# Top-k attention with a gated feed-forward: the 32nd largest score found by a fold into larger and smaller halves

## The chip, the cores and the metric

The kernel runs on one core of one Trainium2 chip. The metric is the device time of one execution in microseconds, the median of several. Of the core's engines five matter here: TensorE (PE, with its weight loads shown apart as PEld), VectorE (DVE), ScalarE (ACT), GpSimd (POOL) and the queues that issue transfers (SP foremost).

## The reference

Attention over 8 batches of 8 heads, 576 tokens and 64 dimensions a head, keeps for each query the 32 largest of its 576 scores; the rest get no weight. Its output, brought into 4608 rows of 512, goes through a feed-forward of 2048 hidden units with the activation h·cos(h). All is float32.

```python
# attention: q, k, v of (8, 8, 576, 64)
scores = scale * np.matmul(q, k.transpose(0, 1, 3, 2))
kth = np.partition(scores, -top_k, axis=-1)[..., -top_k:-top_k + 1]   # top_k = 32
mask = scores >= kth
scores = np.where(mask, scores, -1000000000.0)
scores = scores - np.max(scores, axis=-1, keepdims=True)
attn = np.exp(scores)
attn = attn / (np.sum(attn, axis=-1, keepdims=True) + 1e-09)
out = np.matmul(attn, v)
# feed-forward: x of (4608, 512), w_in (512, 2048), w_out (2048, 512)
h = x @ w_in
g = h * np.cos(h)
y = g @ w_out
```

## The kernel before

The work is cut into 144 units: 128 queries (one to a partition) by two heads. A unit's scores are 2 x 576 numbers a partition. The program is written as slots; in each one, every engine gets a piece of a different unit, and feed-forward pieces ("feed") fill TensorE's time. In the long middle (`slot`), slot i runs the top-k of unit i on VectorE, mask and exponentials of unit i-1 on ScalarE, normalisation and transposition of the units before on GpSimd and by transfers, and scores of unit i+1 on TensorE.

The scores come out in PSUM and are copied to SBUF by ScalarE; after that copy the PSUM tile (one buffer, `bufs=1`) is free for the next unit's scores:

```python
def scores(u):
    sc = u["sc"] = ps.tile([P, 2, 2, 512], F32, tag="sc", name="sc", bufs=1)
    ...
    nc.tensor.matmul(sc[r0 : r0 + rows, j, h, 0:HS], ...)      # HS = 288, h = 0, 1

def take_scores(u):
    s = u["s"] = work.tile([P, 2, S], F32, tag="s", name="s", bufs=4)
    nc.scalar.copy(out=s..., in_=u.pop("sc")...[:, :, 0:HS])
```

The top 32 are found in four rounds. Each takes the eight largest in order (`max`, MAX8 in the profile) and overwrites them by the lowest number (`match_replace`: a MATCH_VALUE_LOAD and a MATCH_REPLACE8), for each of the two heads; the last round needs no replacement. The 32nd value is the threshold, the first is the maximum:

```python
def topk_round(u, rnd):
    s = u["s"]
    if rnd == 0:
        u["m8"] = small.tile([P, 2, TOPK], F32, tag="m8", name="m8")
        u["rest"] = work.tile([P, 2, S], F32, tag="rest", name="rest", bufs=1)
    m8, rest = u["m8"], u["rest"]
    src = s if rnd == 0 else rest
    at = slice(8 * rnd, 8 * rnd + 8)
    for j in range(2):
        nc.vector.max(m8[:, j, at], src[:, j])                                    # L237
    if rnd < TOPK // 8 - 1:
        for j in range(2):
            nc.vector.match_replace(rest[:, j], m8[:, j, at], src[:, j], NEG)     # L240
    else:
        del u["rest"]

def bounds(u):
    m8 = u.pop("m8")
    nb = u["nb"] = small.tile([P, 2, 2], F32, tag="nb", name="nb")
    nc.scalar.mul(out=nb, in_=m8[:, :, 0 : TOPK : TOPK - 1], mul=-SCALE)          # L248
    ...
```

The order of a slot in the middle (z holds two units in every other slot, else nothing):

```python
def slot(i, u, w, x, y, z):
    if x: reciprocal(x)                      # DVE
    if u: topk_round(u, 0); decode_second(2) # DVE
    if w: bounds(w); mask(w); exponentials(w)        # ACT
    if u: topk_round(u, 1); topk_round(u, 2); topk_round(u, 3)   # DVE
    take_banks()                             # ACT: feed-forward banks
    if z: values(z)                          # PE
    if i + 1 < NU: scores(units[i + 1])      # PE
    if z: take_values(z)                     # ACT
    if i + 1 < NU: take_scores(units[i + 1]) # ACT
    ...
    gate(1)                                  # POOL: g * sine(x), L457
    if x: normalise(x); split(x); write_halves(x)    # POOL L282, L294, then SP
    feed(2)                                  # PE: feed-forward
    take_banks()
    ...
    reduce_first(); reduce_second()          # POOL L431 to L433, L440
    feed(3)                                  # PE
    sines(2)                                 # ACT
```

`decode_second` (L137, L138) is part of a decoding of the weights, on VectorE, in the first slots only. In the end, after the last slot, `reduce_first` and `gate` run on VectorE (L423, L426, L457) instead of GpSimd.

Of the kernel before, what the change touches and what calls it, by code (L numbers as in the profile page):

```python
# [10 lines left out]
F32 = mybir.dt.float32  # L11
# [3 lines left out]
AF = mybir.ActivationFunctionType  # L15
ALU = mybir.AluOpType

P = 128
TOPK = 32
NEG = -3.4028234663852886e38  # L20
# [11 lines left out]
def kernel(  # L32
# [9 lines left out]
    nc = tc.nc  # L42
    ctx.enter_context(tc.manual_schedule())
    B, H, D, S = qT.shape
# [6 lines left out]
    HS = S // 2  # L51
    SCALE = 1.0 / math.sqrt(D)
# [5 lines left out]
    work = ctx.enter_context(tc.tile_pool(name="work", bufs=2))  # L58
    small = ctx.enter_context(tc.tile_pool(name="small", bufs=4))
# [25 lines left out]
    for i in range(DF // CW):  # L85
        w = consts.tile([P, NC, CW], F32, tag=f"w_in{i}", name=f"w_in{i}")
        w_in.append(w)
        for c in range(NC):
            cols = slice(words * i * CW, words * (i + 1) * CW)
            chunks.append((moe_w_in[c * P : (c + 1) * P, cols], w[:, c]))  # L90
    for f in range(NF):
        w = consts.tile([P, DM], F32, tag=f"w_out{f}", name=f"w_out{f}")
# [62 lines left out]
    units = []  # L155
    for t0 in range(0, B * S, P):
        parts = []
# [63 lines left out]
    def take_scores(u):  # L221
        s = u["s"] = work.tile([P, 2, S], F32, tag="s", name="s", bufs=4)
        nc.scalar.copy(  # L223
            out=s.rearrange("p j (h w) -> p (j h) w", h=2),
            in_=u.pop("sc").rearrange("p j h w -> p (j h) w")[:, :, 0:HS],
        )

    def topk_round(u, rnd):
        s = u["s"]
        if rnd == 0:  # L230
            u["m8"] = small.tile([P, 2, TOPK], F32, tag="m8", name="m8")
            u["rest"] = work.tile([P, 2, S], F32, tag="rest", name="rest", bufs=1)
        m8, rest = u["m8"], u["rest"]
        src = s if rnd == 0 else rest
# [6 lines that stand above are left out]
        else:  # L241
            del u["rest"]

    def bounds(u):

        m8 = u.pop("m8")
        nb = u["nb"] = small.tile([P, 2, 2], F32, tag="nb", name="nb")
        nc.scalar.mul(out=nb, in_=m8[:, :, 0 : TOPK : TOPK - 1], mul=-SCALE)  # L248
        nd = u["nd"] = small.tile([P, 2], F32, tag="nd", name="nd")
        for j in range(2):  # L250
            nc.scalar.activation(
                out=nd[:, j : j + 1], in_=m8[:, j, TOPK - 1 : TOPK], func=AF.Identity,
                bias=nb[:, j, 0:1], scale=SCALE,
            )

    def mask(u):

        s, nb = u["s"], u.pop("nb")
        for j in range(2):
            nc.scalar.activation(  # L260
                out=s[:, j], in_=s[:, j], func=AF.Prelu, bias=nb[:, j, 1:2], scale=SCALE, alpha=FAR
            )
# [63 lines left out]
    def values(us):  # L326


        o = us[0]["o"] = ps.tile([P, 512], F32, tag="mm", name="o", bufs=4)
        for i, u in enumerate(us):  # L330
            pT = u.pop("pT")
            for b, _, rows, r0 in u["parts"]:
                st = pairs[b, u["hp"]]
                r = slice(r0, r0 + rows)
                to = slice(i * P + r0, i * P + r0 + rows)
                for c in range(NT + 1):
                    for j in range(2):
                        d = slice(j * D, (j + 1) * D)
                        if c < NT:
                            lhsT, rhs = st["v"][:, c, d], pT[:, j * (NT + 1) + c, r]  # L340
                        else:
                            lhsT, rhs = st["v_tail"][:, d], pT[:, NT, r]
                        nc.tensor.matmul(o[d, to], lhsT, rhs, start=c == 0, stop=c == NT)  # L343
# [35 lines left out]
    def ff1(blk, i):  # L379
        w = blk["w"]  # L380
        nf = 256 // w
        part = i % 4
        if part == 0:
            blk["g"].append(ffw.tile([P, 1024], F32, tag="g", name="g", bufs=CHUNKS))
            ff["live"] += 1
        if part % 2 == 0:
            blk["mm"] = ps.tile([P, 512], F32, tag="mm", name="mm", bufs=4)
        g, mm = blk["g"][-1], blk["mm"]
        for a in range(nf):
            f = i * nf + a  # L390
            at = (part % 2 * nf + a) * w
            for c in range(NC):
                nc.tensor.matmul(  # L393
                    mm[:, at : at + w],
                    w_in[f // FC][:, c, (f % FC) * P : (f % FC + 1) * P],
                    blk["xT"][:, c],
                    start=c == 0,
                    stop=c == NC - 1,
                )
        if part % 2 == 0:  # L400
            return
        full.append((take_first, blk, g, mm, part // 2))
# [6 lines left out]
    def take_banks():  # L409
        while full:  # L410
            take, *what = full.popleft()
            take(*what)
# [47 lines left out]
    def ff2(blk, i, f0):  # L460
        w = blk["w"]
        if f0 == 0:
            blk["o"] = ps.tile([P, 512], F32, tag="mm", name="o2", bufs=4)
        o = blk["o"]
        per = 1024 // w
        for f in range(f0, f0 + 2):
            g = blk["g"][f // per]
            at = (f % per) * w + i * P
            nc.tensor.matmul(  # L469
                o, g[:, at : at + P], w_out[f], start=f == 0, stop=f == NF - 1  # L470
            )
        if f0 + 2 < NF:
            return
        full.append((take_second, blk, i, o))
# [25 lines left out]
    def feed(n):  # L500

        ff["tick"] += 1
        while n > 0 and ff["credit"] >= 1:
            for kind in (ff["kind"], 1 - ff["kind"]):
                if (can_first, can_second)[kind]():
                    break
            else:
                return
            if kind == 0:
                ff1(*first.popleft())  # L510
            else:
                ff2(*second.popleft())
            ff["kind"] = 1 - kind
            n, ff["credit"] = n - 1, ff["credit"] - 1
# [10 lines left out]
    for n in range(NP, len(order)):  # L525
        i = last[order[n - 5]] - 1 if n >= 5 else 0
        at_slot.setdefault(max(i, NP + 2), []).append((load_qk, *order[n]))
        i = last[order[n - 6]] if n >= 6 else 0
# [8 lines left out]

    EARLY, LAST = 2 * NP, NU - NP

    def early_slot(i, u, w):  # L540
        n = 3 if i < 6 else 2
        topk_round(u, 0)
        decode_second(1 if i == 0 else n)
        scores(units[i + 1])
        for load, b, hp in at_slot.get(i, []):
            load(b, hp)
        load_weights(n)
        if w:
            bounds(w)
            mask(w)  # L550
            exponentials(w)
            reciprocal(w)
        topk_round(u, 1)
        if i == 0:
            decode_second(2)
        topk_round(u, 2)
        topk_round(u, 3)
        if w:
            normalise(w)
        take_banks()  # L560
        take_scores(units[i + 1])
        gate(1)
        decode_third()
        feed(2)
        reduce_first()
        reduce_second()
        if i != NP:
            decode_first(n - 1)
        if w:
            transposes_now(w)  # L570
        feed(1)
        decode_first(n - len(wq["second"]))
        if w:
            values([w])
            take_values([w])
        feed(2)
        sines(2)

    def slot(i, u, w, x, y, z):
        if x:  # L580
            reciprocal(x)
        if u:
            topk_round(u, 0)
            decode_second(2)
        if w:
            bounds(w)
            mask(w)
            exponentials(w)
        if u:
            topk_round(u, 1)  # L590
            topk_round(u, 2)
            topk_round(u, 3)
        take_banks()
        if z:
            values(z)
        if i + 1 < NU:
            scores(units[i + 1])
        if z:
            take_values(z)
        if i + 1 < NU:  # L600
            take_scores(units[i + 1])
        for load, b, hp in at_slot.get(i, []):
            load(b, hp)
        load_weights(2)
        if y:
            transposes(y)
        gate(1)
        if x:
            normalise(x)
            split(x)  # L610
            write_halves(x)
        feed(2)
        take_banks()
        decode_third()
        decode_first(2)
        reduce_first()
        reduce_second()
        feed(3)
        sines(2)
# [51 lines left out]
    for i in range(NU + 1):  # L671
# [4 lines left out]
        u, w = (units[i - n] if 0 <= i - n < NU else None for n in range(2))  # L676
# [55 lines left out]
```

## Time and profile before

| | |
|---|---|
| time, median of 3 | 1534.06 us (1532.54 to 1536.82) |
| span of the profiled execution | 1530.3 us, 28322 instructions |
| largest groups on GpSimd | L294 copy 2103 ns x132, L440 2372 ns x68, L457 2374 ns x68, L282 750 ns x288 |
| largest group on ScalarE | L268 exponentials 763 ns x288 |
| scores, L213 | 186.9 us busy, x1280 |

The profile is one execution taken by the hardware profiler. Its page gives busy times by engine, the chain of work that ended last, and the costliest groups of instructions: program line, engine, operation, output<-input, shapes, count, then busy us, mean ns of one instruction, and the idle time of the engine in front of them. The trace behind it can be asked for a timeline of one engine, or for busy times by stretch of time ("windows"). The length of an instruction includes latency that overlaps the next one, so what it costs a full engine is read from the distance between starts.

### The profile page before, as it was taken

How to read it: one execution, taken by the hardware profiler on the slowest of the kernel's cores; microseconds unless marked ns; L12 is line 12 of the kernel's file. 1: busy time of each engine (PE TensorE's matmuls, PEld its weight loads, DVE VectorE, ACT ScalarE, POOL GpSimd, SP SyncE). 2: the span in 40 equal slices, each digit the busy share in tenths (PEclk: the TensorE clock that was granted, in tenths of full speed). 3: DMA queues.
4: the chain of work that ended last, by engine and by line, in shares of the span. 5: the costliest groups of instructions: out<-in, count | busy, mean ns of one | idle time of the engine just before them, and what ended most of it. 6: DMA issues, size and time to landing. Idle time of an engine off the chain costs nothing.

```text
span 1530.3 us, 28322 instructions
## 1 busy us (share of the span) xinstructions
PE 1430.3 (93%) x10360; PEld 1022.7 (67%) x10360; DVE 1449.0 (95%) x3102; ACT 1109.6 (73%) x2150; POOL 1105.4 (72%) x838
## 2 busy tenths in 40 slices
PE   4678588999999999999999999999999999999998
PEld 3466266676767676767676767676767676767675
DVE  7999999999999999999999999999999999999911
ACT  7887667777777777777777777777777777777731
POOL 4778957777878787877777777777777778777600
PEclk6588899999999999999999999999999999999999
DMA  8432255645674556655565365645654446444200
GB/s 269 139 96 90 87 152 151 177 116 162 163 178 116 147 133 169 170 132 146 162 170 140 117 162 162 163 131 137 187 148 142 135 131 162 144 136 120 81 8 14
DMA packets 371740, 212.09 MB, mean 139 GB/s; under 512 B 321296, under 2 KB 337937, under 8 KB 371601
## 3 DMA queue, kind: packets, MB, share of 16 engines
q1 hardware_dynamic: 366192, 200.63, 48.4%
q10 hardware_dynamic: 5408, 9.65, 1.7%
q8 instruction: 81, 1.33, 0.4%
q14 instruction: 59, 0.48, 0.1%
HBM read 45.09 MB, written 87.29 MB: 87 GB/s over the span
## 4 chain that ended last, share of the span: by engine, by line
DVE 72%; PE 16%; ACT 5%; issue 5%; DMA 1%; POOL 0%; SPq 0%; ACTq 0%; POOLq 0%; DVEq 0%
DVE m L237 36%; DVE rest L240 33%; PE mm L393 6%; PE o L469 6%; PE o L343 2%; PE sc L213 1%; ACT s L268 1%; ACT s L260 1%; DVE w_out L138 1%; ACT st L127 1%; DVE rden L277 1%; DMA v<-in_v_dram 1%; ACT st L128 0%; PE tp L317 0%; DMA st<-in_moe_w_in_dram 0%
## 5 line engine op out<-in xcount | busy, mean ns | idle before, releaser
L393 PEld LDWEIGHTS mm<-xT,w_in 128*128 128x128 f32 x4608 | 546.6, 193 | 117.0 <-issue 95.2
L237 DVE MAX8 m<-rest 128x8 f32<-128x576 f32 x864 | 613.7, 757 | 0.0
L393 PE MATMUL mm<-xT,w_in 128*128 128x128 f32 x4608 | 567.0, 278 | 19.0 <-ACT xT L349 19.0
L469 PE MATMUL o<-w_out,g 128*128 128x512 f32 x1152 | 539.3, 600 | 11.5 <-POOL g L457 7.5
L240 DVE MATCH_REPLACE8 rest<-m,rest 128x576 f32<-128x576 f32 x576 | 426.4, 753 | 0.0
L469 PEld LDWEIGHTS o<-w_out,g 128*128 128x128 f32 x1152 | 202.7, 191 | 206.2 <-issue 190.7
L294 POOL COPY halves<-s 128x2304 uint16<-128x2304 uint16 x132 | 277.6, 2103 | 85.8 <-DMA rows<-halves 80.1
L282 POOL TENSOR_SCALAR s<-s,rden 128x576 f32<-128x576 f32 x288 | 212.3, 750 | 84.4 <-DVE rden L277 84.4
L268 ACT ACTIVATE s<-s,nd 128x576 f32<-128x576 f32 x288 | 219.5, 763 | 0.6
L240 DVE MATCH_REPLACE8 rest<-m,s 128x576 f32<-128x576 f32 x288 | 213.2, 753 | 0.0
L237 DVE MAX8 m<-s 128x8 f32<-128x576 f32 x288 | 203.1, 752 | 7.0 <-ACT s L223 7.0
L260 ACT ACTIVATE s<-s,nb 128x576 f32<-128x576 f32 x288 | 205.3, 760 | 0.0
L457 POOL TENSOR_TENSOR g<-g,x 128x1024 f32<-128x1024 f32 x68 | 161.4, 2374 | 57.3 <-ACT x L450 57.3
L213 PE MATMUL sc<-k,q 64*128 64x288 f32 (+1 forms) x1280 | 186.9, 439 | 14.5 <-ACT s L223 14.5
L223 ACT COPY s<-sc 128x1152 f32<-128x1152 f32 x144 | 160.6, 1115 | 39.9 <-PE sc L213 39.3
L343 PEld LDWEIGHTS o<-pT,v 128*64 128x64 f32 x2560 | 136.7, 141 | 69.2 <-issue 37.2
L343 PE MATMUL o<-pT,v 128*64 128x128 f32 (+1 forms) x2560 | 165.7, 272 | 14.3 <-ACT pT L321 8.4
L440 POOL TENSOR_TENSOR x<-g,x 128x1024 f32<-128x1024 f32 x68 | 161.3, 2372 | 5.7
L248 ACT ACTIVATE nb<-m 128x4 f32<-128x4 f32 x144 | 29.6, 206 | 185.3 <-DVE m L237 185.3
L405 ACT ACTIVATE g<-mm 128x512 f32<-128x512 f32 x144 | 84.3, 587 | 107.7 <-PE mm L393 107.7
L213 PEld LDWEIGHTS sc<-k,q 64*128 64x128 f32 (+1 forms) x1280 | 101.6, 182 | 66.5 <-ACT s L223 17.6
L431 POOL TENSOR_SCALAR x<-g 128x1024 f32<-128x1024 f32 x68 | 71.1, 1046 | 98.8 <-ACT g L405 94.0
(48 smaller groups left out, 1042.3 us busy)
## 6 DMA issues: line engine op xcount, KB each, us to landing
rows<-halves SPq DMA_DIRECT2D x132, 576.0 KB, 3.2
out_dram<-ob ACTq DMA_DIRECT2D x36, 256.0 KB, 2.1
q<-in_q_dram SPq DMA_DIRECT2D x31, 288.0 KB, 3.1
st<-in_moe_w_in_dram SPq DMA_DIRECT2D x16, 512.0 KB, 5.3
v<-in_v_dram SPq DMA_DIRECT2D x32, 256.0 KB, 3.5
st<-in_moe_w_out_dram SPq DMA_DIRECT2D x16, 512.0 KB, 3.6
k<-in_k_dram SPq DMA_DIRECT2D x31, 144.0 KB, 3.4
k<-in_k_dram SPq DMA_DIRECT2D x32, 128.0 KB, 3.9
```

Of the source, the lines that this page charges most:

```text
L213: nc.tensor.matmul(sc[r0 : r0 + rows, j, h, 0:HS], st["q"][d, q0 : q0 + rows], st["k"][d, h * HS : (h + 1) * HS], start=True, stop=True,)
L237: nc.vector.max(m8[:, j, at], src[:, j])
L240: nc.vector.match_replace(rest[:, j], m8[:, j, at], src[:, j], NEG)
L260: nc.scalar.activation(out=s[:, j], in_=s[:, j], func=AF.Prelu, bias=nb[:, j, 1:2], scale=SCALE, alpha=FAR)
L268: nc.scalar.activation(out=s[:, j], in_=s[:, j], func=AF.Exp, bias=nd[:, j : j + 1], scale=1.0, accum_out=den[:, j : j + 1],)
L282: nc.gpsimd.tensor_scalar(out=s[:, j], in0=s[:, j], scalar1=rden[:, j : j + 1], scalar2=1.0, op0=ALU.mult, op1=ALU.mult,)
L294: nc.gpsimd.tensor_copy(out=halves, in_=s.rearrange("p (k h) -> p h k", h=2))
L343: nc.tensor.matmul(o[d, to], lhsT, rhs, start=c == 0, stop=c == NT)
L393: nc.tensor.matmul(mm[:, at : at + w], w_in[f // FC][:, c, (f % FC) * P : (f % FC + 1) * P], blk["xT"][:, c], start=c == 0, stop=c == NC - 1,)
L440: nc.gpsimd.tensor_tensor(out=x, in0=g, in1=x, op=ALU.subtract)
L457: eng.tensor_tensor(out=g, in0=g, in1=x, op=ALU.mult)
L469: nc.tensor.matmul(o, g[:, at : at + P], w_out[f], start=f == 0, stop=f == NF - 1)
```

## The change

The 576 scores of a query are taken in pairs, score c of the left half with score c of the right half. VectorE writes the larger of each pair into the first 288 columns of `rest` and the smaller into the other 288 (`fold`). A pair can give both of its scores to the top 32 only if its smaller one belongs there, so at most 16 of the smaller ones can. The 32 largest of the larger ones (four rounds) and the 16 largest of the smaller ones (two rounds) therefore hold the top 32, in two ordered lists. The 32nd largest of both lists together is the largest of: the 32nd of the first list, and for n = 1 to 16 the lesser of the first list's entry 32-n and the second list's entry n. That is one `tensor_tensor` minimum, with the first list read backwards, and one reduction. The purpose is that the rounds run over half as many columns.

The left half is read from the PSUM tile of the scores, the right half from its copy in SBUF; the PSUM tile is therefore held until the fold has read it. Units 10 to 141 of 0 to 143 fold, the others keep the four rounds over 576. In slots without values to compute (`z` empty) a feed-forward piece now stands ahead of the next scores.

```diff
+        if not u["folds"]:
+            del u["sc"]          # in take_scores; otherwise the PSUM tile lives on
+
+    def fold(u):
+        s, sc = u["s"], u.pop("sc")
+        rest = u["rest"] = work.tile([P, 2, S], F32, tag="rest", name="rest", bufs=1)
+        for i, op in enumerate((ALU.max, ALU.min)):
+            nc.vector.tensor_tensor(
+                out=rest[:, :, i * HS : (i + 1) * HS], in0=sc[:, :, 0, 0:HS], in1=s[:, :, HS:S],
+                op=op,
+            )
 
     def topk_round(u, rnd):
+        if u["folds"]:
+            return folded_round(u, rnd)
...
+    def folded_round(u, rnd):
+        HALF = TOPK // 2
+        if rnd == 0:
+            fold(u)
+            u["m8"] = small.tile([P, 2, TOPK + HALF + 1], F32, tag="m8", name="m8", bufs=3)
+            u["ends"] = slice(0, TOPK + HALF + 1, TOPK + HALF)
+            u["low"] = small.tile([P, 2, HALF], F32, tag="low", name="low", bufs=1)
+        m8, low, rest = u["m8"], u["low"], u["rest"]
+        parts = [(m8[:, :, 8 * rnd : 8 * rnd + 8], slice(0, HS), rnd < TOPK // 8 - 1)]
+        if rnd < HALF // 8:
+            parts.append((low[:, :, 8 * rnd : 8 * rnd + 8], slice(HS, S), rnd < HALF // 8 - 1))
+        for to, cols, more in parts:
+            for j in range(2):
+                nc.vector.max(to[:, j], rest[:, j, cols])
+            if more:
+                for j in range(2):
+                    nc.vector.match_replace(rest[:, j, cols], to[:, j], rest[:, j, cols], NEG)
+        if rnd < TOPK // 8 - 1:
+            return
+        nc.vector.tensor_tensor(
+            out=m8[:, :, TOPK : TOPK + HALF], in0=m8[:, :, TOPK - 2 : TOPK - 2 - HALF : -1],
+            in1=low, op=ALU.min,
+        )
+        nc.vector.tensor_reduce(
+            out=m8[:, :, TOPK + HALF], in_=m8[:, :, TOPK - 1 : TOPK + HALF],
+            axis=mybir.AxisListType.X, op=ALU.max,
+        )
+        del u["rest"], u["low"]
...
+    for i, u in enumerate(units):
+        u["folds"] = EARLY + 2 <= i < LAST + 2        # EARLY = 8, LAST = 140
...
         take_banks()
         if z:
             values(z)
+        else:
+            feed(1)
         if i + 1 < NU:
             scores(units[i + 1])
```

More of the change, by code (lines that the diff above doesn't have):

```diff
@@ L224, in take_scores @@
             out=s.rearrange("p j (h w) -> p (j h) w", h=2),
-            in_=u.pop("sc").rearrange("p j h w -> p (j h) w")[:, :, 0:HS],
+            in_=u["sc"].rearrange("p j h w -> p (j h) w")[:, :, 0:HS],
         )
+        if not u["folds"]:
[8 more added lines that the diff above has]
+            )
     def topk_round(u, rnd):
+        if u["folds"]:
+            return folded_round(u, rnd)
         s = u["s"]
         if rnd == 0:
-            u["m8"] = small.tile([P, 2, TOPK], F32, tag="m8", name="m8")
+            u["m8"] = small.tile([P, 2, TOPK + TOPK // 2 + 1], F32, tag="m8", name="m8", bufs=3)
+            u["ends"] = slice(0, TOPK, TOPK - 1)
             u["rest"] = work.tile([P, 2, S], F32, tag="rest", name="rest", bufs=1)
@@ L242, in topk_round @@
             del u["rest"]
+    def folded_round(u, rnd):
[26 more added lines that the diff above has]
+        del u["rest"], u["low"]
     def bounds(u):
-        m8 = u.pop("m8")
+        m8, ends = u.pop("m8"), u.pop("ends")
         nb = u["nb"] = small.tile([P, 2, 2], F32, tag="nb", name="nb")
-        nc.scalar.mul(out=nb, in_=m8[:, :, 0 : TOPK : TOPK - 1], mul=-SCALE)
+        nc.scalar.mul(out=nb, in_=m8[:, :, ends], mul=-SCALE)
         nd = u["nd"] = small.tile([P, 2], F32, tag="nd", name="nd")
@@ L251, in bounds @@
             nc.scalar.activation(
-                out=nd[:, j : j + 1], in_=m8[:, j, TOPK - 1 : TOPK], func=AF.Identity,
+                out=nd[:, j : j + 1], in_=m8[:, j, ends.stop - 1 : ends.stop], func=AF.Identity,
                 bias=nb[:, j, 0:1], scale=SCALE,
```

## The prediction

> **What bounds the kernel now.** I read the page first: the table of engines, then the chain that ended last, then the costliest groups. Columns of a group: line, engine, operation, output<-input, shapes, count | busy us, mean ns of one | idle before it.
>
> ```profile
> PE 1430.3 (93%) x10360; PEld 1022.7 (67%) x10360; DVE 1449.0 (95%) x3102; ACT 1109.6 (73%) x2150; POOL 1105.4 (72%) x838
> ...
> DVE 72%; PE 16%; ACT 5%; issue 5%; DMA 1%; POOL 0%; SPq 0%; ACTq 0%; POOLq 0%; DVEq 0%
> ...
> L237 DVE MAX8 m<-rest 128x8 f32<-128x576 f32 x864 | 613.7, 757 | 0.0
> ...
> L240 DVE MATCH_REPLACE8 rest<-m,rest 128x576 f32<-128x576 f32 x576 | 426.4, 753 | 0.0
> ```
>
> Two engines are nearly full, and the chain runs 72% through VectorE (DVE): the top-k rounds, which never wait (idle 0.0). The windows view, cut into stretches, shows the long middle (columns: length, busy us and count for PE, PEld, DVE, ACT, POOL, then PE clock, DMA share, GB/s):
>
> ```profile
> 600.00:800.00 200.00, 198.24 (x1505) 144.36 (x1503) 200.00 (x435) 149.49 (x287) 152.06 (x113) 1.00 0.58 155
> ```
>
> DVE is busy for all 200 us, PE for 198, POOL (GpSimd) for 152. One unit (128 queries, two heads) in the DVE timeline (start us, length, then the instruction):
>
> ```profile
> 741.60 0.17 DVE L277 RECIPROCAL rden<-den 128x2 f32<-128x2 f32 x1
> 741.66 1.42 DVE L237 MAX8 m<-s 128x8 f32<-128x576 f32 x2
> 742.98 0.09 DVE L240 MATCH_VALUE_LOAD rest<-m,s 128x8 f32 x1
> 743.04 0.76 DVE L240 MATCH_REPLACE8 rest<-m,s 128x576 f32<-128x576 f32 x1
> 743.70 0.10 DVE L240 MATCH_VALUE_LOAD rest<-m,s 128x8 f32 x1
> ...
> 751.30 0.16 DVE L277 RECIPROCAL rden<-den 128x2 f32<-128x2 f32 x1
> ```
>
> Reciprocal to reciprocal is 751.30 - 741.60 = 9.70 us, the slot. Starts, not lengths, give what an instruction costs a full engine: two MAX8 from 741.66 to 742.98 are 0.66 each (length 0.76, the last 0.10 overlaps the next); value load 0.06 and MATCH_REPLACE8 0.66 make 0.72. Check: 8 x 0.66 + 6 x 0.72 + 0.06 = 9.66, near 9.70.
>
> PE is close behind. From its timeline in the same slot: 32 feed-forward matmuls of 128 columns at 0.112, 8 of 512 columns at 0.43, scores 1.24, and values 2.33 for two units, so 3.58 + 3.44 + 1.24 + 1.17 = 9.4 us. Even a free DVE could not bring the slot below some 9.4.
>
> [...]
>
> [...] VectorE's timeline and then GpSimd's:
>
> ```profile
> 101.23 0.90 DVE L137 TENSOR_SCALAR w_out<-w_out 128x512 f32<-128x512 f32 x1
> 102.17 2.45 DVE L138 TENSOR_SCALAR w_out<-w_out 128x512 int32<-128x512 int32 x1
> 104.53 0.41 DVE L137 TENSOR_SCALAR w_out<-w_out 128x512 f32<-128x512 f32 x1
> ...
> 101.94 2.39 POOL L440 TENSOR_TENSOR x<-g,x 128x1024 f32<-128x1024 f32 x1
> ```
>
> L138 takes 2.45 instead of 0.43 us [...].
>
> **The change part by part, for one of the 132 units that fold (10 to 141).**
>
> Removed: 8 MAX8 and 6 replacements of 576 wide: 8 x 0.66 + 6 x 0.72 = 9.6 us.
>
> Added, DVE:
> - Two tensor_tensor of 2x288 = 576 elements, one input in PSUM: [...] 660 if PSUM costs no more than SBUF. I take 0.70 each: 1.40. [...]
> - MAX8 of 288 wide: halving 576 elements takes 300 ns off, 0.36 each. 4 rounds x 2 heads on the larger, 2 x 2 on the smaller: 12 x 0.36 = 4.32.
> - Replacements of 288 wide: 0.72 - 0.30 = 0.42. 3 x 2 plus 1 x 2: 8 x 0.42 = 3.39 (0.424 unrounded).
> - The tail is a dependent chain. Back-to-back dependent instructions start 0.04 after the one before ended (1472.78 + 0.69 = 1473.47, the next at 1473.51). The last MAX8 of 288 is 0.46 long instead of 0.36, so the minimum waits 0.14 more; the 32-element tensor_tensor itself is about 0.18 (a reciprocal of 2 elements is 0.16) + 0.04; the reduction of 17 elements each for 2 heads occupies 0.10. Sum 0.46.
> - Reciprocal 0.06.
>
> Sum: 1.40 + 4.32 + 3.39 + 0.46 + 0.06 = 9.63 us. So the elements fall from 14 x 576 = 8064 to 20 x 288 + 2 x 576 = 6912, 1.2 us less[...]. Without a lock: 0.07 x 132 = 9 us gained.
>
> Added wait, the deciding term: the 32-element tensor_tensor (minimum of the two ordered lists) has both inputs in SBUF[...]. It stands on the path: the threshold reduction, the reciprocal and the next fold are behind it on DVE. I laid GpSimd's timeline beside the 128 reciprocals of the middle. 0.25 to 0.5 us ahead of a reciprocal, where this instruction would stand, GpSimd is inside an instruction in 59 to 70% of the slots (the 2.37 us tensor_tensor of L440 and L457, the 2.1 us copy of L294, the 1.05 us L431 to L433), and the mean rest until that instruction ends, idle slots counted as zero, is 0.52 to 0.81 us. A random phase gives the same: squares of the lengths per slot, 2 x 0.75² + 2.1² + 0.47 x (2 x 2.37² + 3 x 1.05²) = 12.4, over twice 10 us, 0.62. I take 0.55, as part of it is latency that the instruction has anyway.
>
> Slot: 9.63 + 0.55 = 10.18, against 9.70: +0.48 x 132 = +63 us.
>
> Moved, PE: the scores' PSUM tile (one buffer) is now held until both fold instructions have read it, about 0.06 + 1.40 + 0.16 = 1.6 us into the slot. Before, PE began the next scores 1.4 us into the slot at the earliest, 2.0 in the tenth percentile, 3.9 in the median. So nearly no slot waits there, and the extra feed before the scores in slots without values gives PE work meanwhile. With a slot of 10.2 PE has 0.8 us to spare. I add 1 us in all. ACT is 73% busy and only follows the threshold. 1534 + 63 + 1 = 1598.
>
> **The rivals.**
> - No lock for so short an instruction, or GpSimd idle at that point because the longer feed shifts its work. For it: a fifth to two fifths of slot ends find GpSimd idle now[...]. Then 9.63 a slot, 1525 us; with the PSUM price at 660 ns 9.55, about 1515. PE's 9.4 stops it there.
> - The fold contends too[...]. Two instructions at the slot's start, where the timeline has GpSimd busy in 88 to 98% of slots with a mean rest of 0.6 to 0.85: at least another 0.7 us a slot, 1690 or more. [...]
> - PE becomes the bound: scores late behind the fold push values and feed-forward late. For it: PE's 198 of 200 us. Against: its latest allowed point is hardly later than where it already works. If every slot lost 0.3 us: 1565.
> - The phases lock badly, each stall leaving GpSimd at the start of a 2.37 us instruction when the next minimum comes: 1.0 us a slot, 1657.
>
> **Range and chances.** The lock at 0.3 to 0.9 us a slot spans 1565 to 1645 and has most of the weight; no lock (1515 to 1535) has about one chance in six, more than 1640 about one in ten. Range 1528 to 1640. Faster by over 2% (under 1503) would need a slot of 9.45, at PE's own limit: 0.02. Within 2% (up to 1565): no lock, or half of it, 0.22. Slower: 0.76.
>
> **What would show it.** In the profile after: MAX8 of 288 at about 457 ns mean and starts 0.36 apart; the fold at 0.70 to 0.73 between starts; the 32-element minimum with a mean near 0.7 us, minimum 0.2, its long ones ending just after a GpSimd instruction ends; reciprocals some 10.2 us apart and uneven, where now they are all within 0.01 of 9.70; PE down to about 90% of the middle. Wrong if the minimum is always 0.2 us (first rival), if the fold is well over 0.75 (second), or if DVE shows idle gaps before the fold on ACT's copy of the scores (third).

## The result and the profile after

The changed kernel takes 1576.0 us (median of 4, 1575.0 to 1576.3) against 1534.6 before: 41 us more, ratio 1.027 (95% interval 1.025 to 1.029). The prediction was 1598, range 1528 to 1640, slower by over 2% at 0.76.

From the page after, in the order of the lines shown of before: engines, chain by engine, costliest groups. L274 are the MAX8, L277 the replacements. The last line is the windows view of the middle, in the columns of before.

```profile
PE 1452.2 (92%) x10360; PEld 1034.7 (66%) x10360; DVE 1482.6 (94%) x4686; ACT 1072.4 (68%) x2120; POOL 1104.6 (70%) x838
...
PE 46%; DVE 34%; ACT 14%; DMA 2%; issue 2%; SPq 1%; ACTq 0%; POOL 0%; POOLq 0%; DVEq 0%
...
L274 DVE MAX8 m<-rest 128x8 f32<-128x288 f32 x1056 | 426.9, 446 | 0.0
L277 DVE MATCH_REPLACE8 rest<-m,rest 128x288 f32<-128x288 f32 x792 | 344.5, 443 | 0.0
...
600.00:800.00 200.00, 192.73 (x1426) 136.93 (x1426) 198.47 (x656) 135.96 (x273) 144.70 (x107) 0.99 0.55 149
```

VectorE has 1584 more instructions, 12 a unit, and is as full as before: 198.5 of 200 us in the middle. The chain, 72% VectorE then, now changes between TensorE, VectorE and ScalarE. The groups of VectorE alone, with the new instructions:

```profile
L236 DVE TENSOR_TENSOR rest<-sc,s 128x576 f32<-128x576 f32 x264 | 185.2, 743 | 1.7 <-ACT s L223 1.2 <-ACT nb L296 0.2 <-issue 0.2
L282 DVE TENSOR_TENSOR m<-m,low 128x32 f32<-128x32 f32 x132 | 84.5, 640 | 4.5
L286 DVE TENSOR_REDUCE m<-m 128x2 f32<-128x34 f32 x132 | 25.3, 191 | 4.5
```

The minimum of 32 elements (L282) takes 640 ns on average, the fold of 576 (L236) 743, the reduction of 34 elements 191. The single instructions of L282 range widely (min/median/max in ns):

```profile
L282 DVE TENSOR_TENSOR m<-m,low x132: 193/208/2294, 152.2 to 1472.8; 128x32 f32<-128x32 f32 x132
```

Half of them are short. Over the shortest, the 132 lose 84.5 - 132 x 0.193 = 59 us: more than the 41 us of the result. VectorE's timeline at the end of two units, one short and one long, and under it GpSimd's at the long one:

```profile
739.95 0.81 DVE L274 MAX8 m<-rest 128x8 f32<-128x288 f32 x2
740.79 0.19 DVE L282 TENSOR_TENSOR m<-m,low 128x32 f32<-128x32 f32 x1
741.02 0.19 DVE L286 TENSOR_REDUCE m<-m 128x2 f32<-128x34 f32 x1
741.13 0.16 DVE L325 RECIPROCAL rden<-den 128x2 f32<-128x2 f32 x1
741.20 1.40 DVE L236 TENSOR_TENSOR rest<-sc,s 128x576 f32<-128x576 f32 x2
742.52 0.81 DVE L274 MAX8 m<-rest 128x8 f32<-128x288 f32 x2
743.25 0.07 DVE L277 MATCH_VALUE_LOAD rest<-m,rest 128x8 f32 x1
743.31 0.44 DVE L277 MATCH_REPLACE8 rest<-m,rest 128x288 f32<-128x288 f32 x1
743.67 0.08 DVE L277 MATCH_VALUE_LOAD rest<-m,rest 128x8 f32 x1
...
759.96 2.04 DVE L282 TENSOR_TENSOR m<-m,low 128x32 f32<-128x32 f32 x1
762.03 0.19 DVE L286 TENSOR_REDUCE m<-m 128x2 f32<-128x34 f32 x1
```

```profile
759.85 2.10 POOL L342 COPY halves<-s 128x2304 uint16<-128x2304 uint16 x1
761.92 2.37 POOL L505 TENSOR_TENSOR g<-g,x 128x1024 f32<-128x1024 f32 x1
```

The long minimum begins 0.1 us after GpSimd's copy and ends at 762.00, with the copy at 761.95. So it is everywhere: 60 of the 132 are over 0.4 us, and each of the 60 ends 37 to 53 ns after a GpSimd instruction ends. The other unit shows the price of the rest, by starts: two fold instructions from 741.20 to 742.52, 0.66 us each; two MAX8 to 743.25, 0.36 each; value load and replacement to 743.67, 0.42. Reciprocals are 9.58 us apart where the minimum is not held, and 10.04 on average (12th to 138th), up to 11.7.

### The profile page after: what moved, and what is told of

It reads as the page before. It is cut to its first block, busy times and chain, and to the rows that moved or that the text cites. A ratio compares the mean times of both kernels' runs of the same rounds, so it can differ in the third digit from the quotient of the medians.

```text
span 1574.3 us, 30010 instructions
## 1 busy us (share of the span) xinstructions
PE 1452.2 (92%) x10360; PEld 1034.7 (66%) x10360; DVE 1482.6 (94%) x4686; ACT 1072.4 (68%) x2120; POOL 1104.6 (70%) x838
## 4 chain that ended last, share of the span: by engine, by line
PE 46%; DVE 34%; ACT 14%; DMA 2%; issue 2%; SPq 1%; ACTq 0%; POOL 0%; POOLq 0%; DVEq 0%
PE mm L441 20%; PE o L517 16%; DVE rest L277 10%; DVE m L274 9%; PE sc L213 5%; PE o L391 5%; DVE low L274 4%; DVE rest L236 4%; ACT s L316 3%; DVE m L282 3%; ACT s L308 2%; ACT x L498 2%; ACT L316 1%; DVE m L253 1%; ACT s L223 1%
## 5 line engine op out<-in xcount | busy, mean ns | idle before, releaser
L441 PEld LDWEIGHTS mm<-xT,w_in 128*128 128x128 f32 x4608 | 553.2, 195 | 133.0 <-issue 95.1
L441 PE MATMUL mm<-xT,w_in 128*128 128x128 f32 x4608 | 575.2, 281 | 32.4 <-ACT xT L397 32.3
L517 PE MATMUL o<-w_out,g 128*128 128x512 f32 x1152 | 548.4, 609 | 3.9 <-POOL w_out L148 3.8
L274 DVE MAX8 m<-rest 128x8 f32<-128x288 f32 x1056 | 426.9, 446 | 0.0
L277 DVE MATCH_REPLACE8 rest<-m,rest 128x288 f32<-128x288 f32 x792 | 344.5, 443 | 0.0
L517 PEld LDWEIGHTS o<-w_out,g 128*128 128x128 f32 x1152 | 206.6, 195 | 204.0 <-issue 195.8
L274 DVE MAX8 low<-rest 128x8 f32<-128x288 f32 x528 | 214.0, 447 | 0.0
L236 DVE TENSOR_TENSOR rest<-sc,s 128x576 f32<-128x576 f32 x264 | 185.2, 743 | 1.7 <-ACT s L223 1.2
L488 POOL TENSOR_TENSOR x<-g,x 128x1024 f32<-128x1024 f32 x68 | 160.9, 2366 | 5.7
L277 DVE MATCH_REPLACE8 rest<-low,rest 128x288 f32<-128x288 f32 x264 | 114.9, 443 | 0.0
```

The costliest lines, as they stand in the source:

```text
L236: nc.vector.tensor_tensor(out=rest[:, :, i * HS : (i + 1) * HS], in0=sc[:, :, 0, 0:HS], in1=s[:, :, HS:S], op=op,)
L274: nc.vector.max(to[:, j], rest[:, j, cols])
L277: nc.vector.match_replace(rest[:, j, cols], to[:, j], rest[:, j, cols], NEG)
L441: nc.tensor.matmul(mm[:, at : at + w], w_in[f // FC][:, c, (f % FC) * P : (f % FC + 1) * P], blk["xT"][:, c], start=c == 0, stop=c == NC - 1,)
L517: nc.tensor.matmul(o, g[:, at : at + P], w_out[f], start=f == 0, stop=f == NF - 1)
```

## Experiments

Before ran again beside each group of runs (1532 to 1535 us); ratios are against those.

| run | what differs | us | ratio to before (95%) |
|---|---|---|---|
| after | | 1576.0 | 1.027 (1.025 to 1.029) |
| e1 | after, minimum as a one-input reduction | 1555.0 | 1.015 (1.013 to 1.016) |
| e2 | before + tiny instruction, two SBUF inputs | 1617.1 | 1.055 (1.053 to 1.056) |
| e3 | before + tiny instruction, one SBUF input | 1550.6 | 1.012 (1.010 to 1.013) |
| e4 | after, without the added feed | 1586.2 | 1.035 (1.033 to 1.037) |
| e5 | after, fold from SBUF alone | 1689.0 | 1.101 (1.099 to 1.102) |
| e6 | e1 and e4 together | 1521.0 | 0.991 (0.990 to 0.993) |
| e7 | before, without the third round's replacements | 1512.6 | 0.986 (0.984 to 0.987) |
| e8 | before + hold of the scores' PSUM tile | 1550.9 | 1.011 (1.009 to 1.012) |
| e9 | e6, reciprocal moved into a gap | 1513.9 | 0.988 (0.986 to 0.990) |
| e10 | before + the added feed | 1556.6 | 1.016 (1.014 to 1.018) |

**The hold by itself: e2 and e3.** Both add one instruction that depends on nothing at the end of the rounds of before, for units 10 to 141. Theory 1 of the expectations is that GpSimd's instruction holds VectorE's when that has two SBUF inputs, in the prediction's word a "lock"; theories 2 and 3 are set out with e1.

```diff
+            if 10 <= u["n"] < NU - NP + 2:
+                dump = small.tile([P, 2, 16], F32, tag="dump", name="dump", bufs=1)
+                # e2: two SBUF inputs
+                nc.vector.tensor_tensor(
+                    out=dump, in0=ident[:, 0:32].rearrange("p (j n) -> p j n", j=2),
+                    in1=ident[:, 32:64].rearrange("p (j n) -> p j n", j=2), op=ALU.min)
+                # e3 instead: one SBUF input
+                nc.vector.tensor_reduce(
+                    out=dump, in_=ident[:, 0:64].rearrange("p (j n l) -> p j n l", j=2, l=2),
+                    axis=mybir.AxisListType.X, op=ALU.min)
```

> The kernel before, with one added 32-element tensor_tensor per unit 10 to 141 at the end of its four rounds, both inputs from a constant in SBUF, result unused: it depends on nothing. Theory 1 [...]: it is held as the minimum is; GpSimd is busy at 82% of these points with a mean rest of 0.89 us, so 0.5 to 0.9 us a slot with its own 0.10: 1534 + 132 x 0.6 to 1.0 = 1613 to 1665 us. Theory 2 or 3: only its own 0.10 us a slot, 1547 us.

> The same as the one with two inputs, but the added instruction is a tensor_reduce over 64 elements of the constant (one SBUF input, the same 32 results). Theory 1: never held, its own 0.13 us a slot, 1534 + 17 = 1551 us. Theory 3 (any short instruction at this place is held): like the one with two inputs.

The groups of VectorE, e2 and then e3:

```profile
L248 DVE TENSOR_TENSOR dump<-ident 128x32 f32<-128x32 f32 x132 | 95.0, 720 | 0.0
```

```profile
L248 DVE TENSOR_REDUCE dump<-ident 128x32 f32<-128x64 f32 x132 | 33.7, 255 | 0.0
```

The one-input instruction adds its own 0.13 us to each slot (9.83 between reciprocals, all within 0.02) and lands on the 1551 expected. GpSimd is inside an instruction at the start of 92 of the 132, and none is held: the longest takes 307 ns. The one with two inputs, which writes as many results, costs 67 us more. It depends on no other engine's result, so what holds it is no data; 79 of the 132 are over 0.4 us, each ending 34 to 53 ns after a GpSimd instruction. The two differ in the operation too, but that is not it: the fold is the operation of e2, and with one input in PSUM none of its 264 takes more than 759 ns (in e5 below, with both in SBUF, some take 2.9 us). The 1617 of e2 is at the low end of its range: the hold is 0.55 us a slot beyond e3, where the unheld phases of before gave a mean rest of 0.89. The phases shift once VectorE is held.

**The hold taken out of the change: e1.** The smaller list is stored backwards in the same tile, 34 places on, so that partners lie at one stride and a reduction over pairs can take the minimum.

```diff
-            parts.append((low[:, :, 8 * rnd : 8 * rnd + 8], slice(HS, S), rnd < HALF // 8 - 1))
+            at = 2 * TOPK - 8 * rnd          # m8 is 2 * (TOPK + 2) = 68 wide here
+            parts.append((m8[:, :, at : at - 8 : -1], slice(HS, S), rnd < HALF // 8 - 1))
...
-        nc.vector.tensor_tensor(
-            out=m8[:, :, TOPK : TOPK + HALF], in0=m8[:, :, TOPK - 2 : TOPK - 2 - HALF : -1],
-            in1=low, op=ALU.min,
+        nc.vector.tensor_reduce(
+            out=m8[:, :, TOPK : TOPK + HALF],
+            in_=m8.rearrange("p j (l w) -> p j w l", l=2)[:, :, HALF - 1 : TOPK - 1],
+            axis=mybir.AxisListType.X, op=ALU.min,
         )
```

> The changed kernel, but the 32-element minimum of the two lists is a tensor_reduce over pairs (64 elements, one SBUF input) instead of a tensor_tensor with two SBUF inputs. Theory 1 [...]: the long ones vanish, reciprocals are 9.62 us apart (9.58 in unheld slots plus 0.03 for 32 more elements), time about 1524 us (9.70 - 9.62 = 0.08 x 132 = 11 us under before). Theory 2 (the time goes to TensorE, whose scores wait behind the fold for the PSUM tile): nothing changes, about 1576 us. Theory 3 (the wait is for something else that ends late, and the next instruction takes it over): about 1576 us, with the wait in front of the reduction or the reciprocal.

```profile
L236 DVE TENSOR_TENSOR rest<-sc,s 128x576 f32<-128x576 f32 x264 | 186.2, 747 | 26.1 <-ACT s L223 24.7 <-issue 0.4
L282 DVE TENSOR_REDUCE m<-m 128x32 f32<-128x64 f32 x132 | 29.2, 221 | 4.5
```

The minimum is 221 ns, always, and where VectorE does not wait, reciprocals are 9.61 to 9.62 us apart, as theory 1 had it. But only 21 of 59 us came back: VectorE now waits 26 us in front of the fold, for ScalarE's copy of the scores, in place of 1.7. None of the three theories foresaw that a second, hidden limit stood just behind the hold. The waits view, before and then e1, leads on (waiter <- releaser: us, times, longest):

```profile
ACT s L223 <- PE sc L213: 39.3, 54, 3.8
```

```profile
ACT s L223 <- PE sc L213: 166.8, 84, 4.1
```

TensorE makes the scores late, 5.5 to 7.6 us into most slots, against 1.5 to 4.8 before, and the copy waits for them. What VectorE loses by it comes for the most part in one slot of eight, 0.8 to 1.3 us there. ScalarE's timeline from the copy of one slot to that of the next in such a place, then VectorE's and TensorE's:

```profile
670.42 1.12 ACT L223 COPY s<-sc 128x1152 f32<-128x1152 f32 x1 [2.00 <-PE sc L213]
671.56 1.28 ACT L499 ACT_TABLE_LOAD   x1
672.85 2.19 ACT L499 ACTIVATE x<-x,halfpi 128x1024 f32<-128x1024 f32 x2
...
677.00 1.28 ACT L317 ACT_TABLE_LOAD   x1
...
680.15 0.58 ACT L527 ACTIVATE ob<-o 128x512 f32<-128x512 f32 x1
680.76 0.34 ACTq L529 DMA_DIRECT2D out_dram<-ob  x1
681.14 0.37 ACT L398 COPY xT<-o 128x256 f32<-128x256 f32 x1 [0.41 <-ACT ob L527]
681.41 1.12 ACT L223 COPY s<-sc 128x1152 f32<-128x1152 f32 x1
```

```profile
682.57 1.42 DVE L236 TENSOR_TENSOR rest<-sc,s 128x576 f32<-128x576 f32 x2 [0.90 <-ACT s L223]
```

```profile
679.10 0.71 PE L442 MATMUL mm<-xT,w_in 128*128 128x128 f32 x4
681.57 1.60 PE L442 MATMUL mm<-xT,w_in 128*128 128x128 f32 x12 [1.76 <-ACT xT L398]
```

The first copy waits 2.00 us for late scores. Behind it ScalarE works through two sines, the exponentials, two table loads, an output and xT with 0.54 us of idle time in 9.88, and only then comes the next copy, which waits for nothing but its place in this queue. A slot of VectorE is 9.61. The feed-forward of TensorE, which needs xT, stands still behind the same queue; such a pause need not cost anything: before has it too in these places, 0.7 to 1.3 us, and VectorE does not wait there. Two suspects for the late scores: the added feed ahead of them, and the PSUM tile held until the fold.

**The tile's hold and the feed apart: e8, e10, e4, e6.**

```diff
# e8, before: nothing else reads the tile after the copy
+        sc = u.pop("sc", None)
+        if sc is not None and 10 <= u["n"] < NU - NP + 2:
+            dump = small.tile([P, 2, 16], F32, tag="dump", name="dump", bufs=1)
+            nc.vector.tensor_reduce(
+                out=dump, in_=sc[:, :, 0, 0:32].rearrange("p j (n l) -> p j n l", l=2),
+                axis=mybir.AxisListType.X, op=ALU.min)
```

```diff
# e10: added to before.   e4: taken out of after.   e6: taken out of e1.
         if z:
             values(z)
+        else:
+            feed(1)
         if i + 1 < NU:
             scores(units[i + 1])
```

> The kernel before, with the PSUM tile of the scores held until a small tensor_reduce (64 elements of it) at the start of the unit's rounds has read it; result unused. Theory A (holding the tile is free while VectorE sets the slot): only the 0.13 us of the added instruction, as the one-input one at the end of the rounds, 1550 us. Theory B (the hold keeps TensorE from working ahead and costs of itself): 1560 us or more, with TensorE's scores waiting for the reduction.

> The kernel before, with the added feed-forward piece ahead of the scores in slots without values and nothing else changed. In the reduction variants that piece cost 34 us (1555 against 1521), in the changed kernel it saved 10 (1576 against 1586). Theory A (it costs of itself, through later scores and a wait of TensorE for xT): 1545 to 1565 us, VectorE waiting for the copy of the scores. Theory B (it costs only together with the held PSUM tile): 1535 us.

> The changed kernel without the added feed-forward piece ahead of the scores in slots without values. Theory 1: the feed matters only through where GpSimd stands when the minimum comes; still 0.3 to 0.9 us of hold a slot, 1560 to 1620 us. Theory 2 (scores wait behind the fold and TensorE sets the slot): TensorE has less to do ahead of the scores and the time rises by 10 to 40 us with waits of the scores on the fold. Rival: the moved feed itself cost the 41 us, then 1535 us.

> The variant with the reduction as minimum (1555 us), without the added feed-forward piece ahead of the scores. Theory A (that piece sets TensorE's pace: scores came 5.5 to 7.6 us into the slot there, 1.5 to 4.8 before): scores come early again, slot 9.62 to 9.70, 1522 to 1535 us. Theory B (the PSUM tile held until the fold sets TensorE's pace): TensorE waits for the fold, 1560 to 1580 us.

e8 costs what e3 costs, 1550.9 against 1550.6: this hold, of the PSUM tile, is free. It ends some 0.3 us into the slot, though, where the fold holds the tile for 1.5; that the longer hold is nearly free too is shown by e6, in which TensorE's scores wait for the fold once in the whole run, 5.1 us. e10 costs 24 us with nothing else changed, and its first MAX8 waits for the copy of the scores as e1's fold does (before, then e10):

```profile
L237 DVE MAX8 m<-s 128x8 f32<-128x576 f32 x288 | 203.1, 752 | 7.0 <-ACT s L223 7.0
```

```profile
L237 DVE MAX8 m<-s 128x8 f32<-128x576 f32 x288 | 202.4, 744 | 22.8 <-ACT s L223 22.4
```

So it is the feed. From 200 to 1400 us of e10 VectorE waits 16.2 us for the copy, and 13.3 of these end with a copy that stood in ScalarE's queue and did not itself wait for scores, as in e1. In both, two sines lie between the copies of such a place, where before and e6 have one. That the price comes by way of this queue is read from the timelines; no run tested it by itself. e6, which drops the feed from e1, falls by 34 us to 1521 and is faster than before; the waits view shows the copy's wait back at a third (it was 166.8), and reciprocals are 9.61 to 9.62 us apart in nearly every slot:

```profile
ACT s L223 <- PE sc L213: 55.7, 81, 3.2
```

In the changed kernel the same feed saved 10 us (e4 1586, after 1576). The parts do not add: from e6's 1521, the minimum's hold alone costs 65 (e4), the feed alone 34 (e1), both together 55. In after, VectorE hardly waits for the copies (1.7 us): held behind GpSimd, it comes late enough for the copy, so the feed's price is hidden. And the minimums are held less than without the feed, 59 us against 70 (724 ns mean in e4, 132 x 0.531), as GpSimd then stands elsewhere when they come. Why the feed makes GpSimd stand elsewhere was not taken apart.

**The fold with two SBUF inputs: e5.**

```diff
-                out=..., in0=sc[:, :, 0, 0:HS], in1=s[:, :, HS:S],
+                out=..., in0=s[:, :, 0:HS], in1=s[:, :, HS:S],
```

> The changed kernel, but the fold reads both halves from the SBUF copy, so its two tensor_tensor have two SBUF inputs each and the PSUM tile is not held. Theory 1 [...]: the larger is held behind the GpSimd instruction that starts as the minimum ends, the smaller behind the next; 0.7 to 1.6 us a slot more, 1665 to 1790 us, GpSimd held as well. Theory 2 (the hold of the PSUM tile costs more than the lock): the time falls under 1576 us.

The groups of VectorE, then its timeline at one fold and GpSimd's:

```profile
L236 DVE TENSOR_TENSOR rest<-s 128x576 f32<-128x576 f32 x264 | 298.7, 1172 | 0.9 <-ACT s L223 0.5 <-issue 0.4
```

```profile
702.24 4.34 DVE L236 TENSOR_TENSOR rest<-s 128x576 f32<-128x576 f32 x2
706.50 0.81 DVE L274 MAX8 m<-rest 128x8 f32<-128x288 f32 x2
```

```profile
702.07 1.04 POOL L481 TENSOR_SCALAR x<-x 128x1024 f32<-128x1024 f32 x1
703.20 2.75 POOL L488 TENSOR_TENSOR x<-g,x 128x1024 f32<-128x1024 f32 x1
705.91 2.88 POOL L505 TENSOR_TENSOR g<-g,x 128x1024 f32<-128x1024 f32 x1
```

The pair shown takes 4.34 us where it takes 1.40 with one half in PSUM. 79 of the 264 are held, and a held one ends 0.60 to 0.62 us after GpSimd's instruction. Between starts, MAX8 takes 0.66 us at 576 wide (before) and 0.36 at 288 (after), so 288 elements take 0.30, and a pass over 576 an estimated 0.60 us: by this estimate, the instruction starts on its data only when GpSimd has ended. The hold works in the other direction too: L488 takes 2.75 us here, where the 68 of after take 2.35 to 2.40. The price of not reading one half from PSUM is 1689 - 1576 = 113 us.

**TensorE's own limit: e7.** The third round's replacements are left out, so the fourth finds the third's eight again and the threshold is the 24th score instead of the 32nd.

```diff
-            for j in range(2):
+            for j in range(0 if rnd == 2 and 10 <= u["n"] < NU - NP + 2 else 2):
                 nc.vector.match_replace(rest[:, j], m8[:, j, at], src[:, j], NEG)
```

> The kernel before, with the replacements of the third round left out for units 10 to 141 (the fourth round then finds the same eight again, so the threshold is the 24th score): 2 x 0.72 = 1.44 us less VectorE work a slot, 8.26 us. It shows what TensorE alone allows. By the prediction's 9.4 us: 9.70 - 9.4 = 0.3 x 132 = 40 us less, 1494 us. If TensorE's work with its waits is some 9.6 to 9.7 us a slot, as in the variant with the reduction: 1520 to 1532 us.

The windows view of e7 (PE, PEld, DVE, ACT, POOL busy):

```profile
600.00:800.00 200.00, 200.00 (x1545) 146.31 (x1545) 173.42 (x353) 149.91 (x295) 156.40 (x116) 1.00 0.58 152
```

TensorE is busy all 200 us and VectorE 173. With 1.44 us less VectorE work a slot, a slot is 9.53 us on average and the time falls by 22 us, not by 40. That is about all that any change to VectorE can bring while the order of TensorE's work stays.

**A version that beats both: e9.** In e6 the slot is 9.61, VectorE's sum. The minimum waits 0.12 us for the last MAX8; the next slot's reciprocal, whose input has been there for long, fits into that gap.

```diff
+        if "then" in u:                      # the unit whose reciprocal the next slot needs
+            reciprocal(u.pop("then"))
         nc.vector.tensor_reduce(             # the minimum
...
+        if u and u["folds"] and EARLY <= i - 1 < LAST:      # in slot
+            u["then"] = w
...
-        if x:
+        if x and "rden" not in x:
             reciprocal(x)
```

> The variant with the reduction as minimum and without the added feed (1521 us), with the next slot's reciprocal moved from the start of the slot into the gap of 0.12 us in which the minimum waits for the last MAX8. If VectorE sets the slot (9.61): 0.064 us less, 9.55, 1521 - 8 = 1513 us. If TensorE already does (its own pace was 9.53 where VectorE had less to do): 1516 to 1521 us, with VectorE waiting for the scores' copy.

Its timeline at one slot's end:

```profile
702.68 0.14 DVE L328 RECIPROCAL rden<-den 128x2 f32<-128x2 f32 x1
702.80 0.22 DVE L284 TENSOR_REDUCE m<-m 128x32 f32<-128x64 f32 x1
703.05 0.19 DVE L289 TENSOR_REDUCE m<-m 128x2 f32<-128x34 f32 x1
703.16 1.41 DVE L236 TENSOR_TENSOR rest<-sc,s 128x576 f32<-128x576 f32 x2
```

1513.9 us, where 1513 was expected: 7 us under e6, or 5 if each is taken against the runs of before beside it; 1.2% under before (0.988, 0.986 to 0.990). Slots are 9.55 us, 0.02 above those of e7, and TensorE is busy in all 200 us of the same window.

## Why the prediction was right, and where its sizes were off

- **The sum without the hold: 9.63 us a slot predicted, 9.58 measured.** MAX8 at 0.36 between starts (0.30 under the 0.66 of 576 wide), value load and replacement at 0.42, and the dependent tail (0.45 from the end of the last MAX8's 0.36 to the reciprocal, against 0.46) are as worked out. The fold's 0.70 was the author's estimate, above the 0.66 that before shows for 576 elements. Measured, it is 0.66: an input in PSUM cost no more than one in SBUF (lengths of 733 to 759 ns, median 746; with both in SBUF, in e5, from 735, median 751).
- **The deciding term: 0.55 us a slot predicted, 10.04 - 9.58 = 0.46 measured** (59 us over 132 in the instruction's own lengths). That the minimum waits for GpSimd was the author's estimate, not shown by before: the only VectorE instructions there that combine two tensors (L426, L457) come after 1473 us, and GpSimd is done at 1465. What before shows are L137 and L138: 14 of the 64 take over 0.5 us, up to 2.47, and each of the 14 ends 0.28 to 0.29 us after a GpSimd instruction. They read one tensor, though, and why they are held was not shown. For the minimum the wait is shown by e2 against e3 (67 us), by e1 (a mean of 221 ns in place of 640) and e6, and by where the long ones end (37 to 53 ns after a GpSimd instruction). The size came from where GpSimd stood in before; where that is shifts with every change of the schedule, by as much as the 0.09 missed (0.53 in e4, 0.55 in e2).
- Together, (9.58 + 0.46) - 9.70 = 0.34 a slot, times 132 = 45 us, against 63 predicted; the span grew by 44.
- **"The extra feed before the scores ... gives PE work meanwhile", 1 us in all: wrong as a cost.** By itself it is 24 us (e10): it delays the scores, and with them ScalarE's queue, which the prediction passed over with "ACT is 73% busy and only follows the threshold". Beside the minimum's hold it came out as a saving of 10 (e4); that the total does not show the error is luck.
- **The PSUM hold: nearly free as predicted** (e8, and e6 for its full length).
- **"Even a free DVE could not bring the slot below some 9.4": right in kind, low by 0.13.** Measured: 9.53 (e7). What the sum of TensorE's parts leaves out was not taken apart.
- **No lock** (first rival) would have missed too. It said 1525 for the change as it stands; with the hold taken out that is 1555 (e1), and 1521 only with the feed taken out as well (e6).
- **The fold contending** (second rival) did not happen. With both halves in SBUF it did, at 1689 (e5), where the rival had said 1690 or more; that the two agree so closely is luck, as the rival added 92 us to 1598 and e5 adds 113 to 1576.
- **PE as the bound** (third rival) did not happen in after, where VectorE waits 1.7 us in front of the fold. Its sign, VectorE idle there for the copy of the scores, came in e1 with 26 us, but from the feed and not from scores that stand behind the fold.
- **"PE down to about 90% of the middle": wrong.** After, it is 192.7 of 200 us in the same window, 96%. A slot's matmuls are 9.61 us of busy time before and 9.67 after (198.24 / 200 x 9.70 and 192.73 / 200 x 10.04), not the 9.4 of their paces, and in e7 they fit into 9.53. Busy TensorE time counts more than the work needs; leaving work out of VectorE was the safer gauge.

## What to carry to other kernels

On an engine that sets the pace, a short instruction is not cheap because it is short: here one of 0.2 us cost 0.64 on average. Ask how many of its inputs lie in SBUF while GpSimd works beside it, and give it one (a strided reduction over pairs, 0.22 us and never held) or put the other into PSUM (the fold, none of 264 over 0.76 us); one input alone is no guarantee, as L137 and L138 of before show. Halving the width does not halve an instruction: MAX8 went from 0.66 to 0.36 us between starts, by which some 60 ns do not shrink with it (an estimate, 2 x 0.36 - 0.66). Here 1152 fewer elements a unit, against twelve more instructions at some 60 ns each and a dependent tail, left 14 us of 1534. And before valuing such a gain, measure the next limits: with work left out of VectorE, TensorE stood 22 us behind, and a reordering of TensorE's work cost more than the fold could bring, by the traces through ScalarE, which was busy for only 69% of the span (e1).

## What was not expected of the hardware

- A fold instruction with one input in PSUM and one in SBUF took 0.66 us for 576 elements, as did one with both in SBUF where it was not held (e5). A reduction of 64 elements from PSUM alone made a slot 0.12 us longer (e8), from SBUF 0.13 (e3).
- The hold ends sharply: a held 32-element instruction ends 34 to 53 ns after the GpSimd instruction, a held 576-element one 0.60 to 0.62 us after.
- The minimum's hold and the feed cost 65 and 34 us alone and 55 together: two limits that take turns hide each other's price.
